# Attention into a three-way-max FFN on one core: weight conversion in three steps, and what the ledger books

## The chip, the cores and the metric

The kernel runs on one core of a Trainium2 chip. Its time is the device time of one execution in microseconds (us), taken from the start of the program to its end. Runs of the same kernel are compared by their median; the trace comes from one execution under the hardware profiler, whose own time stands beside its span below. The core has TensorE (PE in the profile, PEld for its weight loads), VectorE (DVE), ScalarE (ACT), GpSimd (POOL) and SyncE (SP), which here issues all DMA transfers.

## The reference

A local attention with some global tokens, followed by a feed-forward network. There are 8 batches and 8 heads of 512 local and 32 global tokens, of 64 elements each. A local token attends to the 32 global tokens and to the local ones at most 32 places away; a global token attends to all 544.

```python
k_all = concatenate([k_g, k_l], axis=2);  v_all = concatenate([v_g, v_l], axis=2)
out_g = sm(scale * q_g @ k_all.T) @ v_all
s_ll  = where(abs(i - j) <= 32, scale * q_l @ k_l.T, -1e9)
s_lg  = scale * q_l @ k_g.T
out_l = sm(concatenate([s_lg, s_ll], -1)) @ v_all          # sm: softmax
x     = concatenate([out_g, out_l], axis=2)                # to 4608 tokens x 512
h     = maximum(maximum(x @ w1, x @ w2), x @ w3)           # 512 x 768 weights
out   = h @ w_out                                          # 768 x 512
```

All is float32, apart from the four weight arrays, which are float64 in the memory.

## The kernel before

**Precision.** Nearly every product is made of three TensorE products in the fast float32 format (`F32R`): each operand is split into a high part (a cast to `F32R`) and a low part (the operand less the high part), and high x high, high x low and low x high are added in PSUM. A split thus is a cast (`copy`, lines L100 or L102) and a subtraction (`sub`, L94). The first 28 score tiles and 26 probability tiles are instead computed in plain float32 with one product (`NATK`, `NAT`).

**Attention.** A tile `sl` is 128 local queries of a pair `p` of heads; there are 4 tiles a pair (`t`), 16 a batch and 128 in all. For a tile, `scores` makes two score halves on PE (L307 plain, L311 split); a custom DVE operation (L314) adds the mask and takes the maximum `nm`; ACT takes the exponential with its sum (L316); the reciprocal (L318, L319) and a scaling (`times`, L108 DVE, L110 ACT or L112 POOL) give the probabilities `s`, which go through a DMA (L322) to a buffer `early` (tiles up to 15) or `prob`. `trans` transposes them on PE (L334) and splits the result into `pt`; `transg` does so for the global tokens' probabilities (L355); `pv` multiplies by V (L375 plain, L382 split) into `xr`. `glob` and `glob_soft` are scores and softmax of the global queries of the next pair: PE at L265 and L269, DVE's maximum `nmg` at L273. `split_k`, `split_q` and `split_v` make the parts of K, Q and V.

**FFN.** Once the four pairs of a batch are done, `split_x` splits the FFN's input, and `moe_local(b - 1)` is worked off in small portions of matmuls (`fill(4)`, `fill(4)`, `fill(3)`, `fill(7)`) between the steps of the attention tiles of the next batch. For each of 6 column blocks f there are 36 matmuls (L413) with maxima on DVE (L421), then come 4 x 18 matmuls with `w_out` (L432). After the last tile the FFN of the last batch and of the global tokens follows alone.

**Weights.** There are 24 pieces of 128 x 512: 18 of w1, w2, w3 (three for each f) and 6 of `w_out`. A piece is loaded as raw 64-bit words (`wraw`, L162), and `convert` makes a float32 of it by bit operations: ACT's absolute value (L167), then four DVE operations (L168 to L171) into `cut` or, for `w_out`, `wct`; then the high part `wh` or `woh` by `copy` and the low part `wl` or `wol` by `sub`. `convert` is a generator, and `weight_step` moves it on: two steps a piece, and one step carries the second half of one piece and the first of the next. The table `WS` gives the number of steps behind each of tiles 0 to 25.

**What sets the order.** Three things. `copy`, `sub` and `times` choose their engine by a ledger: `load` holds the ns booked for ACT, DVE and POOL, `least` takes the engine with the smallest sum, `spend` books the work that has a fixed engine, and `settle` limits how far an engine can fall behind. Second, each engine works off its own list in order, as the program is written; up to the transpose of tile 16 (`EARLY`) the scheduler of the framework orders the instructions by its own rules. Third, buffers are reused, so a load waits for the last reader of what lay there: `wraw` shares its buffers with the FFN's `h`, `kraw` has one buffer and `kst` two.

Of the kernel before, what the change touches and what calls it, by code (L numbers as in the profile page):

```python
# [10 lines left out]
F32R = mybir.dt.float32r  # L11
# [3 lines left out]
ALU = mybir.AluOpType  # L15
# [4 lines left out]
DM, DF = 512, 768  # L20
# [27 lines left out]
def f32(ap):  # L48
    return ap.bitcast(F32)


def body(ctx, tc, kin, qin, vin, min_, w1, w2, w3, w4, out):
# [23 lines left out]
    def spend(e, ns):  # L76
        load[e] += ns
# [18 lines left out]
    def copy(out, a, psum=False):  # L96
        n = width(out)
        c = {"d": n * (1.04 if psum else 0.52) + (160 if psum else 150), "a": n * 0.833 + (150 if psum else 190)}
        if least(c) == "d":
            dve.tensor_copy(out=out, in_=a)  # L100
        else:
            act.copy(out=out, in_=a)  # L102
# [32 lines left out]
    wo = []  # L135
# [3 lines left out]
    def pieces():  # L139
        n = 0  # L140
        for f in range(12):
            for i in range(3 if f < 6 else 1):
                if f < 6:
                    src = (w1, w2, w3)[i][:, f * 128:(f + 1) * 128].rearrange("(k p) f -> p k f", p=128)
                    yield src, 4, n, wh[f][:, i].rearrange("p k f -> p (k f)"), wl[f][:, i].rearrange("p k f -> p (k f)")
                else:
                    if f == 6:
                        wo.extend(const.tile([128, 6, DM], F32R, name=t, tag=t) for t in ("woh", "wol"))
                    yield w4[(f - 6) * 128:(f - 5) * 128], 1, n, wo[0][:, f - 6], wo[1][:, f - 6]
                n += 1  # L150

    def STAGE(n):
# [5 lines left out]
    def convert(piece):  # L158
        src, k, m, dh, dl = piece
        n, i = 512, STAGE(m)  # L160
        r = moe.tile([128, n], mybir.dt.int64, name="wraw", tag=f"h{i}")
        nc.sync.dma_start(out=r.rearrange("p (k f) -> p k f", k=k) if k > 1 else r, in_=src)  # L162
        hi = r.bitcast(I32).rearrange("p (n t) -> p n t", t=2)[:, :, 1]
        lo = r.bitcast(I32).rearrange("p (n t) -> p n t", t=2)[:, :, 0]
        yield
        c = cut[:, m % 6] if m < 18 else moe.tile([128, n], I32, name="wct", tag="o", bufs=2)
        act.activation(out=f32(c), in_=r.bitcast(F32).rearrange("p (n t) -> p n t", t=2)[:, :, 1], func=AF.Abs)  # L167
        dve.tensor_scalar(out=f32(c), in0=f32(c), scalar1=2.0 ** -15, scalar2=HIMAX, op0=ALU.max, op1=ALU.min)  # L168
        dve.tensor_scalar(out=c, in0=c, scalar1=0x07FFFFFF, scalar2=3, op0=ALU.bitwise_and, op1=ALU.logical_shift_left)
        dve.scalar_tensor_tensor(out=hi, in0=hi, scalar=-0x40000000, in1=c, op0=ALU.bitwise_and, op1=ALU.bitwise_or)  # L170
        dve.scalar_tensor_tensor(out=c, in0=lo, scalar=29, in1=hi, op0=ALU.logical_shift_right, op1=ALU.bitwise_or)  # L171
        spend("a", 520)
        spend("d", 1900)
        yield
        copy(dh, f32(c))
        sub(dl, f32(c), f32(dh))
        yield

    todo = pieces()
    live = []  # L180
# [8 lines left out]


    def weight_step():
        if live:
            next(live.pop())
        if loaded:
            live.append(loaded.pop(0))
            next(live[0])
        weight_load()


# [54 lines left out]
    def glob(p, step):  # L254
        if p >= B * NP:
            return
        if step == 0:
            pg[p] = [att.tile([64, KW], F32, name="sg", bufs=1)[:, 0:NG], small.tile([64, 2], F32, name="nmg"), small.tile([64, 2], F32, name="zg")]
        s, nm, z = pg[p]
        c0, n = SEG[step]  # L260
        s0 = 384 * step
        ps = psS.tile([128, 512], F32, name="S")
        if 4 * p in NATK:

            pe.matmul(ps[0:64, 0:n], lhsT=kraw[p][:, KW:KW + 2 * SG], rhs=kraw[p][:, c0:c0 + n], start=True, stop=True)  # L265
            in1 = zero[0:64].to_broadcast([64, n])
        else:
            for j in range(2):
                pe.matmul(ps[:, 0:n], lhsT=qgz.rearrange("p j x -> p (j x)")[:, 128 * j:128 * j + 128],  # L269
                          rhs=kst[p][:, j, c0:c0 + n], start=(j == 0), stop=(j == 1))  # L270
            in1 = s[:, s0:s0 + n]
            copy(in1, ps[64:128, 0:n], True)
        dve.tensor_tensor_reduce(out=s[:, s0:s0 + n], in0=ps[0:64, 0:n], in1=in1, scale=-0.125, scalar=3.0e38,  # L273
                                 op0=ALU.add, op1=ALU.min, accum_out=nm[:, step:step + 1])
        spend("d", n * 1.04 + 75)

    def glob_soft(p):
        if p >= B * NP:
# [13 lines left out]
    def scores(sl):  # L292
        if sl >= NS:
            return
        p, t = divmod(sl, 4)
        c0, n = WIN[t]

        ps = pm.tile([128, 512], F32, name="pm") if sl < 12 else psS.tile([128, 512], F32, name="S")
        s = att.tile([128, 2, 224], F32, name="s", bufs=4)
        sc[sl] = early[:, sl % 6] if sl < EARLY else prob[sl % 2]  # L300
        nm = small.tile([128, 2], F32, name="nm")
        z = small.tile([128, 2], F32, name="z")
        ph = [ps[:, 0:224], ps[:, 224:448]]
        for j in range(2):
            if sl in NATK:

                pe.matmul(ph[j][:, 0:n], lhsT=qraw[sl][:, 128 * j:128 * j + 128], rhs=kraw[p][:, c0:c0 + n],  # L307
                          start=True, stop=True)
                continue
            for a in range(2):  # L310
                pe.matmul(ph[j][:, 0:n], lhsT=qs[sl][:, a, 128 * j:128 * j + 128],  # L311
                          rhs=kst[p][:, j, c0:c0 + n], start=(a == 0), stop=(a == 1))
        for j in range(2):
            dve.tensor_tensor_reduce(out=s[:, j, 0:n], in0=ph[j][:, 0:n], in1=mask[:, (1, 0, 1, 0)[t], 32 * (t == 0):32 * (t == 0) + n],  # L314
                                     scale=-0.125, scalar=3.0e38, op0=ALU.add, op1=ALU.min, accum_out=nm[:, j:j + 1])
            act.activation(out=s[:, j, 0:n], in_=s[:, j, 0:n], func=AF.Exp, bias=nm[:, j:j + 1], scale=-1.0,  # L316
                           accum_out=z[:, j:j + 1])
        dve.tensor_scalar(out=z, in0=z, scalar1=1e-9, scalar2=None, op0=ALU.add)  # L318
        dve.reciprocal(out=z, in_=z)  # L319
        for j in range(2):  # L320
            times(s[:, j, 0:n], s[:, j, 0:n], z[:, j:j + 1])
        nc.sync.dma_start(out=f32(sc[sl])[:, :, 0:n], in_=s[:, :, 0:n])  # L322
        spend("d", 2 * (n * 1.04 + 75) + 150)
        spend("a", 2 * (n * 0.833 + 278))

    def trans(sl):
# [171 lines left out]
    for sl in range(NS):  # L498
        p, t = divmod(sl, 4)
# [5 lines left out]
        trans(sl + 1)  # L505
        fill(4)
        next_scores(max(min(sl + 5, EARLY - 1), sl + 3))
        if t == 3:
            split_k(p + 2)
            load_k(p + 3)  # L510
        fill(4)
# [72 lines left out]
```

## Time and profile before

| | |
|---|---|
| median of 3 runs | 871.46 us (870.19 to 872.28) |
| the profiled execution's own time | 868.76 us |
| its span | 867.0 us |
| mean granted TensorE clock | 0.968 of full speed |
| busy: PE | 817.3 us, 94% |
| busy: DVE | 617.3 us, 71% |
| busy: ACT | 492.0 us, 57% |
| busy: POOL | 502.9 us, 58% |
| chain that ended last | PE 77%, DVE 10%, DMA 6% |

The busy times are shares of the whole span. The span has three parts: up to about 85 us there is attention alone and weights are converted; up to about 757 us attention tiles and FFN matmuls alternate; the last 110 us are FFN alone. In rows of the timeline the start in us comes first, then the duration, the engine, the line and the operation, and in brackets the idle time of the engine before it and what ended that. In rows of groups the busy time in us and the mean duration in ns stand behind the count.

### The profile page before, as it was taken

To read this page: it belongs to the slowest core of one execution; us is meant where nothing else is said; L and a number is where in the kernel's file an instruction comes from. 1 tells how busy PE (TensorE), PEld (TensorE's weight loads), DVE (VectorE), ACT (ScalarE), POOL (GpSimd) and SP (SyncE) were. 2 spreads that over 40 slices of the span, in tenths; PEclk is the share of its full clock that TensorE was granted. 3 is DMA by queue.
4 is the path that set the end of the run, shared out by engine and by line. 5 is a ranking of instruction groups with operands and counts; after the bars stand their busy time and mean duration, and the time that the engine had idled before them with its cause. 6 is when DMAs were issued, how large, how long until landed. Compare 5 with 4: busy or idle time off the path is not lost.

```text
span 867.0 us, 15698 instructions
## 1 busy us (share of the span) xinstructions
PE 817.3 (94%) x4452; PEld 677.3 (78%) x4452; DVE 617.3 (71%) x1885; ACT 492.0 (57%) x1392; POOL 502.9 (58%) x669
## 2 busy tenths in 40 slices
PE   5865988799999999999999999999999999999997
PEld 3643766588888788888887888888888888888897
DVE  4678897887788787887788887877877877521111
ACT  3654655566666566766666666666666666411111
POOL 4544657576667666776767666756677665411211
PEclk8876889899999999999999999999999999999999
DMA  6676755334333533343333433353333422100000
GB/s 202 192 222 197 212 182 158 117 93 144 99 101 104 160 110 105 99 133 114 103 107 104 142 102 98 101 161 104 111 110 122 122 78 74 62 24 1 25 25 25
DMA packets 107238, 98.53 MB, mean 114 GB/s; under 512 B 21008, under 2 KB 97936, under 8 KB 107152
## 3 DMA queue, kind: packets, MB, share of 16 engines
q1 hardware_dynamic: 107152, 97.53, 37.0%
q8 instruction: 36, 0.59, 0.3%
q14 instruction: 50, 0.41, 0.2%
HBM read 56.85 MB, written 8.91 MB: 76 GB/s over the span
## 4 chain that ended last, share of the span: by engine, by line
PE 77%; DVE 10%; DMA 6%; issue 2%; POOL 2%; ACT 1%; SPq 1%; DVEq 0%; POOLq 0%; ACTq 0%
PE pm L413 45%; PE pm L432 13%; PE O L382 6%; PE S L311 5%; PE T L334 3%; DMA wraw<-w_in 1%; DMA wraw<-wo_in 1%; PE S L269 1%; DVE wraw L170 1%; DVE xs L100 1%; PE S L265 1%; PE S L355 1%; PE O L375 1%; DVE s L314 1%; DVE kst L94 1%
## 5 line engine op out<-in xcount | busy, mean ns | idle before, releaser
L413 PE MATMUL pm<-xs,wh 128*128 128x512 f32 (+1 forms) x1296 | 411.2, 390 | 0.0
L413 PEld LDWEIGHTS pm<-xs,wh 128*128 128x128 f32 x1296 | 235.3, 191 | 31.6
L413 PE MATMUL pm<-xs,wl 128*128 128x512 f32 (+1 forms) x648 | 254.9, 393 | 0.0
L112 POOL TENSOR_SCALAR s<-s,z 128x224 f32<-128x224 f32 (+1 forms) x243 | 111.6, 472 | 87.7 <-ACT lox L102 46.7
L316 ACT ACTIVATE s<-s,nm 128x192 f32<-128x192 f32 (+1 forms) x256 | 118.0, 462 | 48.6 <-DVE nm L314 44.0
L413 PEld LDWEIGHTS pm<-xs,wl 128*128 128x128 f32 x648 | 123.6, 191 | 23.5 <-issue 2.4
L432 PE MATMUL pm<-woh,h 128*128 128x512 f32 x408 | 135.2, 400 | 1.3 <-POOL h L94 1.1
L94 POOL TENSOR_TENSOR h<-m,h 128x512 fp32r<-128x512 f32 (+1 forms) x54 | 69.3, 1284 | 99.2 <-ACT h L102 99.2
L94 POOL TENSOR_TENSOR qs<-qraw,qs 128x256 fp32r<-128x256 f32 x100 | 79.5, 795 | 68.6 <-ACT qs L102 42.0
L421 DVE TENSOR_TENSOR m<-pm,m 128x512 f32<-128x512 f32 (+1 forms) x108 | 71.0, 657 | 63.0 <-PE pm L413 62.7
L94 DVE TENSOR_TENSOR pt<-T,pt 128x512 fp32r<-128x512 f32 x102 | 70.4, 691 | 36.2 <-ACT pt L102 33.8
L432 PEld LDWEIGHTS pm<-woh,h 128*128 128x128 f32 x408 | 74.6, 188 | 15.4 <-POOL h L94 4.3
L314 DVE CUSTOM_DVE_ANT_0 s<-S,mask 128x192 f32<-128x192 f32 (+1 forms) x232 | 77.5, 370 | 9.9 <-PE S L307 5.2
L432 PE MATMUL pm<-wol,h 128*128 128x512 f32 x204 | 81.7, 401 | 0.0
L94 POOL TENSOR_TENSOR vs<-vraw,vs 128x256 fp32r<-128x256 f32 x102 | 75.7, 743 | 9.0 <-ACT vs L102 4.2
L102 ACT CAST pt<-T 128x512 fp32r<-128x512 f32 x83 | 48.4, 583 | 47.6 <-PE T L334 47.6
L382 PEld LDWEIGHTS O<-pt,vs 128*128 128x128 f32 x408 | 66.4, 188 | 9.2
L382 PE MATMUL O<-pt,vs 128*128 128x320 f32 (+1 forms) x408 | 72.8, 299 | 0.0
L102 ACT CAST qs<-qraw 128x256 fp32r<-128x256 f32 x85 | 34.6, 407 | 64.3 <-PE S L311 64.0
L334 PEld LDWEIGHTS T<-identr,prob 128*128 128x128 f32 x448 | 51.3, 143 | 24.9 <-issue 5.0
L311 PEld LDWEIGHTS S<-kst,qs 128*128 128x128 f32 x400 | 59.5, 190 | 11.2 <-DVE nmg L273 2.8
L102 ACT CAST h<-m 128x512 fp32r<-128x512 f32 (+1 forms) x54 | 32.3, 597 | 60.5 <-DVE m L421 60.4
(99 smaller groups left out, 1340.5 us busy)
## 6 DMA issues: line engine op xcount, KB each, us to landing
vraw<-v_in SPq DMA_DIRECT2D x128, 128.0 KB, 2.6
qraw<-q_in SPq DMA_DIRECT2D x100, 128.0 KB, 2.2
prob<-s SPq DMA_DIRECT2D x56, 224.0 KB, 2.4
prob<-s SPq DMA_DIRECT2D x56, 192.0 KB, 2.3
wraw<-w_in SPq DMA_DIRECT2D x18, 512.0 KB, 4.5
out_dram<-o SPq DMA_DIRECT2D x32, 256.0 KB, 2.6
kraw<-k_in SPq DMA_DIRECT2D x25, 320.0 KB, 3.1
qn<-q_in SPq DMA_DIRECT2D x28, 128.0 KB, 3.5
```

The source lines that it names most:

```text
L94: (dve if least(c) == "d" else pool).tensor_tensor(out=out, in0=a, in1=b, op=ALU.subtract)
L100: dve.tensor_copy(out=out, in_=a)
L102: act.copy(out=out, in_=a)
L112: pool.tensor_scalar(out=out, in0=a, scalar1=col, scalar2=1.0, op0=ALU.mult, op1=ALU.mult)
L311: pe.matmul(ph[j][:, 0:n], lhsT=qs[sl][:, a, 128 * j:128 * j + 128], rhs=kst[p][:, j, c0:c0 + n], start=(a == 0), stop=(a == 1))
L314: dve.tensor_tensor_reduce(out=s[:, j, 0:n], in0=ph[j][:, 0:n], in1=mask[:, (1, 0, 1, 0)[t], 32 * (t == 0):32 * (t == 0) + n], scale=-0.12 ...
L316: act.activation(out=s[:, j, 0:n], in_=s[:, j, 0:n], func=AF.Exp, bias=nm[:, j:j + 1], scale=-1.0, accum_out=z[:, j:j + 1])
L334: i = pe.transpose(pr[:, 256 * j + 128 * c:256 * j + 128 * c + 128], s[:, j, 128 * c:128 * c + 128], identr)
L382: pe.matmul(o[:, j, 0:320].rearrange("p (a q) -> p a q", a=2)[:, :, 0:n], lhsT=vs[sl][:, 2 * j + c].rearrange("p a d -> p (a d)"), rhs=pt[ ...
L413: pe.matmul(ps[:, 0:n], lhsT=w[f][:, i, k], rhs=xs[k][:, a, 0:n], start=(q == 0), stop=(q == 11))
L421: dve.tensor_tensor(out=m[:, 0:n], in0=ps[:, 0:n], in1=m[:, 0:n], op=ALU.max)
L432: pe.matmul(ps, lhsT=hh[f][:, a, 128 * t:128 * t + 128], rhs=w[:, f], start=(q == 0), stop=(q == 17))
```

## The change

Three things are changed.

`convert` now has three steps behind the load: ACT's absolute value; the four DVE operations and the high part, which is always a DVE cast; the low part, which is always a POOL subtraction. `weight_step` moves on every piece that is under way by one step. The pair of tiles for `w_out` is made at the first DVE step that needs it.

The ledger books more for DVE in `scores` (for a tile of width n, 2 x (1.04 n + 220) + 440 instead of 2 x (1.04 n + 75) + 150, which is 580 ns more) and in `glob` (145 ns more); for a piece it books 650 ns on ACT, 2800 on DVE and 1350 on POOL as the steps come.

`split_k(p + 2)` and `load_k(p + 3)` stand at the third tile of a pair instead of the fourth.

```diff
@@ convert
         yield
         c = cut[:, m % 6] if m < 18 else moe.tile([128, n], I32, name="wct", tag="o", bufs=2)
         act.activation(out=f32(c), in_=r.bitcast(F32)..., func=AF.Abs)
+        spend("a", 650)
+        yield
         dve.tensor_scalar(out=f32(c), in0=f32(c), scalar1=2.0 ** -15, scalar2=HIMAX, op0=ALU.max, op1=ALU.min)
         dve.tensor_scalar(out=c, in0=c, scalar1=0x07FFFFFF, scalar2=3, ...)
         dve.scalar_tensor_tensor(out=hi, in0=hi, scalar=-0x40000000, in1=c, ...)
         dve.scalar_tensor_tensor(out=c, in0=lo, scalar=29, in1=hi, ...)
-        spend("a", 520)
-        spend("d", 1900)
+        if m >= 18:
+            if not wo:
+                wo.extend(const.tile([128, 6, DM], F32R, name=t, tag=t) for t in ("woh", "wol"))
+            dh, dl = [w[:, dh] for w in wo]
+        dve.tensor_copy(out=dh, in_=f32(c))
+        spend("d", 2800)
         yield
-        copy(dh, f32(c))
-        sub(dl, f32(c), f32(dh))
-        yield
+        pool.tensor_tensor(out=dl, in0=f32(c), in1=f32(dh), op=ALU.subtract)
+        spend("p", 1350)
+        yield True
@@ weight_step
-        if live:
-            next(live.pop())
+        for c in live[:]:
+            if next(c, True):
+                live.remove(c)
         if loaded:
             live.append(loaded.pop(0))
-            next(live[0])
+            next(live[-1])
         weight_load()
@@ glob
-        spend("d", n * 1.04 + 75)
+        spend("d", n * 1.04 + 220)
@@ scores
-        spend("d", 2 * (n * 1.04 + 75) + 150)
+        spend("d", 2 * (n * 1.04 + 220) + 440)
@@ the loop over tiles
-        if t == 3:
+        if t == 2:
             split_k(p + 2)
             load_k(p + 3)
```

In the changed kernel the conversion stands at L165 (absolute value), L168 to L171, L176 (high part) and L180 (low part), and lines from `scores` on have numbers higher by 6.

By count over the whole program DVE has fewer instructions (1808 instead of 1887), ACT more (1171 instead of 1106) and POOL more (688 instead of 674); PE and SP have as many as before. On DVE there are 24 high parts of weights instead of 6; in return K's casts go from 24 to 4, K's subtractions from 7 to 0, Q's casts from 15 to 0 and V's from 17 to 7.

Three places show how rows move. First DVE around the scores of tile 16 (the two halves of width 192). Before, from the second half on:

```order
L314 ISA s,nm<-S,mask 128x192
L314 ISA nm 128x1
L273 ISA sg,nmg<-S,zero 64x160
L273 ISA nmg 64x1
L281 TENSOR_TENSOR nmg<-nmg 64x1
L168 TENSOR_SCALAR cut<-cut 128x512
L169 TENSOR_SCALAR cut<-cut 128x512
L318 TENSOR_SCALAR z<-z 128x2
L314 ISA s,nm<-S,mask 128x224
L314 ISA nm 128x1
L170 SCALAR_TENSOR_TENSOR wraw<-wraw,cut 128x512
L319 RECIPROCAL z<-z 128x2
```

and now:

```order
L320 ISA s,nm<-S,mask 128x192
L320 ISA nm 128x1
L279 ISA sg,nmg<-S,zero 64x160
L279 ISA nmg 64x1
L287 TENSOR_TENSOR nmg<-nmg 64x1
L324 TENSOR_SCALAR z<-z 128x2
L325 RECIPROCAL z<-z 128x2
L320 ISA s,nm<-S,mask 128x224
L320 ISA nm 128x1
L168 TENSOR_SCALAR cut<-cut 128x512
```

The sum and the reciprocal `z` of tile 16 now follow each other directly; three conversion operations and a half of the next tile that stood between or ahead of them come later.

The second place is PE where the FFN starts, from the P·V of tile 16 on. Before:

```order
L375 MATMUL O<-pt,vraw 64x160 x4
L334 MATMUL T<-identr,prob_93 128x128 x4
L413 MATMUL pm<-xs,wh_102 128x512 x2
L413 MATMUL pm<-xs,wl_108 128x512
L413 MATMUL pm<-xs,wh_102 128x512 x2
L355 MATMUL S<-identr,probg_94 128x128
```

and now:

```order
L381 MATMUL O<-pt,vraw 64x160 x4
L419 MATMUL pm<-xs,wh_102 128x512 x2
L419 MATMUL pm<-xs,wl_108 128x512
L419 MATMUL pm<-xs,wh_102 128x512 x2
L419 MATMUL pm<-xs,wl_108 128x512
L419 MATMUL pm<-xs,wh_102 128x512 x2
L419 MATMUL pm<-xs,wl_108 128x512
L419 MATMUL pm<-xs,wh_102 128x512 x2
L419 MATMUL pm<-xs,wl_108 128x512
L419 MATMUL pm<-xs,wh_102 128x512 x2
L340 MATMUL T<-identr,prob_93 128x128 x4
```

Fourteen FFN matmuls have moved ahead of the transpose of tile 17 (`prob_93`).

The third place is DVE at the first split tiles, 155 to 163 us in the trace. Before:

```order
L314 ISA nm 128x1
L100 CAST qs<-qraw 128x256
L100 CAST kst<-kraw 64x576
L94 TENSOR_TENSOR kst<-kraw,kst 64x576
L318 TENSOR_SCALAR z<-z 128x2
L100 COPY sg<-S 64x384
L319 RECIPROCAL z<-z 128x2
L100 CAST vs<-vraw 128x4x64
L108 TENSOR_SCALAR s<-s,z 128x192 x2
L273 ISA sg,nmg<-S,sg 64x384
```

and now:

```order
L320 ISA nm 128x1
L169 TENSOR_SCALAR wct<-wct 128x512
L170 SCALAR_TENSOR_TENSOR wraw<-wraw,wct 128x512
L171 SCALAR_TENSOR_TENSOR wct<-wraw 128x512
L324 TENSOR_SCALAR z<-z 128x2
L279 ISA sg,nmg<-S,sg 64x384
L279 ISA nmg 64x1
L176 CAST woh<-wct 128x512
```

The casts of Q, K and V, K's subtraction, the copy of the global scores and the scaling have left DVE here; three conversion operations of a `w_out` piece stand in their place.

More of the change, by code (lines that the diff above doesn't have):

```diff
@@ L146, in pieces @@
                 else:
-                    if f == 6:
-                        wo.extend(const.tile([128, 6, DM], F32R, name=t, tag=t) for t in ("woh", "wol"))
-                    yield w4[(f - 6) * 128:(f - 5) * 128], 1, n, wo[0][:, f - 6], wo[1][:, f - 6]
+                    yield w4[(f - 6) * 128:(f - 5) * 128], 1, n, f - 6, None
                 n += 1
```

## The prediction

> **What bounds the kernel now.** I read three views. First the busy tenths of the page, 40 slices of 21.7 us:
>
> ```profile
> PE   5865988799999999999999999999999999999997
> DVE  4678897887788787887788887877877877521111
> PEclk8876889899999999999999999999999999999999
> ```
>
> From the ninth slice on TensorE is at nine tenths in every slice but the last, at full clock. Before it PE is at five to eight tenths and its clock dips three times. So the question is what the first 180 us do, and whether the rest keeps its cover. The second view is a table of stretches (window, length, busy us of PE, PEld, DVE, ACT, POOL with their instruction counts, granted clock, DMA share, GB/s):
>
> ```profile
> 70.00:90.00 20.00, 12.61 (x67) 9.43 (x65) 17.81 (x44) 12.10 (x34) 9.47 (x9) 0.67 0.62 194
> 90.00:115.00 25.00, 23.77 (x128) 17.81 (x127) 22.31 (x53) 14.43 (x37) 16.14 (x17) 0.96 0.75 230
> 135.00:155.00 20.00, 17.82 (x99) 13.27 (x98) 13.44 (x38) 10.75 (x28) 13.30 (x15) 1.00 0.48 148
> 155.00:163.70 8.70, 6.08 (x36) 4.76 (x37) 8.54 (x18) 3.84 (x12) 7.55 (x7) 1.00 0.39 119
> 163.70:170.50 6.80, 4.69 (x15) 3.22 (x14) 5.67 (x18) 3.28 (x11) 2.56 (x5) 0.50 0.24 72
> 600.00:700.00 100.00, 99.70 (x551) 83.95 (x550) 81.55 (x256) 66.05 (x190) 68.11 (x93) 1.00 0.37 112
> ```
>
> In the last row PE idles 0.3 of 100 us: work moved from DVE to ACT or POOL is worth nothing there, whatever its size. In 70 to 90 PE idles 7.39 of 20 us at clock 0.67 while DVE is 89% busy; in 155 to 163.7 PE idles 2.62 us while DVE is 98% busy; behind that come 6.8 us at half clock. The third view, PE's waits in 70 to 200 us (total, times, longest), says what ends them, and the timeline where:
>
> ```profile
> PE T L334 <- DMA prob<-s: 8.0, 3, 4.5
> PE S L355 <- DVE nm L314: 3.0, 2, 2.1
> PE S L269 <- DVE nmg L273: 1.9, 1, 1.9
> ...
> 79.94 0.72 PE L334 MATMUL T<-identr,prob 128*128 128x128 f32 x4 [4.50 <-DMA prob<-s]
> 86.43 0.72 PE L334 MATMUL T<-identr,prob 128*128 128x128 f32 x4 [2.89 <-DMA prob<-s]
> 86.95 1.18 PE L413 MATMUL pm<-xs,wh 128*128 128x512 f32 x2
> 148.20 0.26 PE L355 MATMUL S<-identr,probg 128*128 128x128 f32 x1 [2.06 <-issue]
> 155.73 0.28 PE L355 MATMUL S<-identr,probg 128*128 128x128 f32 x1 [0.85 <-DVE nm L314]
> 162.94 0.46 PE L269 MATMUL S<-kst,qgz 128*128 128x160 f32 x2 [1.89 <-DVE nmg L273]
> 166.50 0.37 PE L355 MATMUL S<-identr,probg 128*128 128x128 f32 x1 [2.11 <-DVE nm L314]
> ```
>
> Two places carry the prediction: the two transposes at 79.94 and 86.43, which wait for a probability tile to come back through DMA before the FFN's first matmul at 86.95, and the three waits on DVE at 155.73, 162.94 and 166.50, together 4.85 us. PE waits there for maxima that DVE reaches late, because conversions and splits lie before them in its queue.
>
> **The change, part by part.** The sum is made against the profiled execution's own 868.76 us; the median of the runs, 871.46, lies 2.70 above it, and I add that at the end.
>
> *Tile 16's probabilities (the 4.50 us wait).* Its scale factor is made here:
>
> ```profile
> 73.76 0.43 DVE L168 TENSOR_SCALAR cut<-cut 128x512 f32<-128x512 f32 x1
> 73.98 0.19 ACT L316 ACTIVATION_READ_ACCUMULATOR s<-s,nm 128x1 f32 x1
> 75.55 0.16 DVE L319 RECIPROCAL z<-z 128x2 f32<-128x2 f32 x1
> 75.87 1.54 POOL L112 TENSOR_SCALAR s<-s,z 128x192 f32<-128x192 f32 x2 [5.95 <-ACT cut L167]
> ```
>
> ACT's sum is there at 74.17, yet the reciprocal starts at 75.55, behind two conversion operations, another tile's score half and a third conversion operation. In the new order sum and reciprocal follow each other at once: 74.17 plus an addition, which I take as long as the reciprocal's 0.16, is 74.3, so 1.2 us earlier. POOL had been idle 5.95 us and starts at once. Two casts more ahead of tile 16's scores, by the counts of the two orders, cost 0.3 net. I take -0.9; ends -1.8 (from 73.76) and 0.
>
> *The FFN ahead of tile 17's transpose (the 2.89 us wait).* Fourteen FFN matmuls now stand ahead of that transpose. At the 0.59 us of the row at 86.95 they last 8.3 us, which covers 2.89 wholly. What is late next: tile 17's transpose, by up to 8.3 - 2.89 = 5.4 us, and with it its P·V and what DVE copies from it. DVE is 89% busy in the stretch behind (22.31 of 25), so not all of it stays. I take -2.0; ends -2.9 and 0.
>
> *DVE at 155 to 163 us.* What stands between the tile's last maximum and the global one:
>
> ```profile
> 155.59 0.82 DVE L100 CAST qs<-qraw 128x256 fp32r<-128x256 f32 x1
> 156.33 0.99 DVE L100 CAST kst<-kraw 64x576 fp32r<-64x576 f32 x1
> 157.35 1.74 DVE L94 TENSOR_TENSOR kst<-kraw,kst 64x576 fp32r<-64x576 f32 x1
> 159.74 0.56 DVE L100 COPY sg<-S 64x384 f32<-64x384 f32 x1
> 160.29 1.03 DVE L100 CAST vs<-vraw 128x256 fp32r<-128x256 f32 x1
> 161.25 1.05 DVE L108 TENSOR_SCALAR s<-s,z 128x192 f32<-128x192 f32 x2
> ...
> 159.76 1.41 POOL L94 TENSOR_TENSOR kst<-kraw,kst 64x576 fp32r<-64x576 f32 x1
> ...
> L169 DVE TENSOR_SCALAR wct<-wct 128x512 int32<-128x512 int32 x6 | 2.7, 444 | 0.1
> L170 DVE SCALAR_TENSOR_TENSOR wraw<-wraw,wct 128x512 int32<-128x512 int32 x6 | 4.1, 682 | 0.0
> L171 DVE SCALAR_TENSOR_TENSOR wct<-wraw 128x512 int32<-128x512 int32 x6 | 5.5, 914 | 0.0
> ```
>
> All six leave DVE at this place: 0.82 + 0.99 + 1.74 + 0.56 + 1.03 + 1.05 = 6.19. Three steps of a weight piece come in: 0.44 + 0.68 + 0.91 = 2.04. DVE is 4.15 us earlier at the global maximum, which covers 0.85 + 1.89 and 1.4 of the 2.11 behind them. What is late next is POOL: it is busy 7.55 of 8.70, and one K subtraction more, 1.41 by its own row, is 0.26 more than its room of 1.15. ACT has room (3.84 of 8.70) for the casts. Splitting K one tile sooner gives POOL a tile more time for it; the order leaves the K loads and the last three weight loads at their places among SP's transfers, so that by itself I price at nothing. If that cover is gone, one subtraction of 1.41 stands in front of the scores. I take -4.15 + 0.26 = -3.9; ends -4.85 and 0.
>
> *The half clock behind it.* In 163.7 to 170.5 PE's 4.69 busy us ran at 0.50; at full clock they are 2.35. The dip follows the waits of 1.89 and 2.11; but the 2.06 at 148.20 was followed by none (1.00 in 135 to 155), so shorter waits don't decide it alone. I take half, -1.2; ends -2.35 and 0.
>
> [...]
>
> *Batch boundaries.* There, in 200 to 760 us, PE waits on the subtraction of h and on a global maximum:
>
> ```profile
> PE pm L432 <- POOL h L94: 1.1, 2, 0.9
> PE S L311 <- DVE nmg L273: 0.8, 3, 0.3
> ```
>
> K's cast and subtraction leave DVE in front of these, but the subtraction goes to POOL, in front of h. Ends -1.9 (both waits gone) and +1.4 (one subtraction ahead of one h). I take -1.0, since POOL is a third free in the steady rows (68.11 of 100).
>
> *More casts on DVE.* Eighteen pieces' high parts leave ACT for DVE; some twelve of them fall in 73 to 135 us, where DVE has least room:
>
> ```profile
> L168 DVE TENSOR_SCALAR cut<-cut 128x512 f32<-128x512 f32 x18 | 12.9, 718 | 3.5 <-ACT cut L167 3.4
> L100 DVE CAST wh<-cut 128x512 fp32r<-128x512 f32 x6 | 2.5, 420 | 0.1
> L100 DVE COPY xr<-O 128x160 f32<-128x160 f32 x5 | 1.6, 321 | 1.1 <-PE O L375 1.0
> 111.01 3.00 DVE L168 TENSOR_SCALAR cut<-cut 128x512 f32<-128x512 f32 x1
> ...
> 112.44 1.28 POOL L94 TENSOR_TENSOR wl<-cut,wh 128x512 fp32r<-128x512 f32 x1
> ```
>
> 12 x 0.42 = 5.04, less four xr copies of 0.32 that leave it, is 3.7 us more. DVE's idle time in the first two stretches is 2.19 + 2.69 = 4.9, part of it waiting for scores that come sooner now, so a third is absorbed and I take +2.5. The lower end is 0 (all absorbed). For the upper end: the L168 step takes 0.43 alone and 0.718 on average, so each cast may be stretched by the same 0.29 beside a running POOL; 12 x (0.42 + 0.29) - 1.3 = +7.2, nothing absorbed.
>
> *Free edits.* That ACT no longer stands still for a cut, and that a piece takes a step more, cost and gain nothing: by the table of steps, pieces finish at least a tile before the FFN asks for their column block, and no FFN matmul waits for a weight in the list of PE's waits.
>
> Sum: -0.9 - 2.0 - 3.9 - 1.2 - 1.0 + 2.5 = -6.5, so 862.3 for a profiled execution and **865.0** as the median.
>
> **The rivals.** *A, the waits change hands.* PE gets to the FFN earlier, but the scores come no sooner since DVE sets them (89% in 70 to 115), and what PE saves at 86 and 162 it waits for later. Then tile 16, tile 17, the DVE place and the clock give 0, the casts fall into PE's waits, the boundaries -1.0: 870.5, no change. For it: DVE's share. Against it: at 155 to 163 work really leaves DVE.
>
> *B, DVE's queue from 73 to 135 us becomes the bound: slower.* Place: the score maxima between the conversions. Price: +7.2, as above; PE then waits for probabilities and both early gains are gone; -3.9 and -1.0 stay: +2.3, or **873.8**. It decides from the point where DVE is more than 3.9 + 1.0 = 4.9 us late at 135. For it: the 3.00 us of one L168 while POOL was at work; against it: the order puts the score halves of tiles 17 and 18 nearer together, with fewer conversion steps between.
>
> [...]
>
> *C, everything at its end.* The clock stays up, both early waits and all boundary waits go, the casts are absorbed: -1.8 - 2.9 - 4.85 - 2.35 - 1.9 = -13.8, or **857.7**. For it: 7.39 us of idle PE at 0.67 in one stretch. Against it: six things at once.
>
> **How the numbers follow.** Chances: the forecast 0.55, A 0.17, B 0.16, C 0.12. The forecast's own range is 860 to 869 (the DVE place and the casts half of their way to their ends). The range of 857 to 875 takes in C and B up to 1 us past its price; outside it remain the tails of both. What can be told from no change is 0.2%, 1.7 us: the forecast, C and a small part of A (0.01) are faster, 0.68; the rest of A is the same, 0.16; B is slower, 0.16.
>
> **What would show it.** In the changed profile: FFN matmuls ahead of tile 17's transpose, no wait of 2.9 us there, and the first wait below 4.50 by about 0.9. Between 150 and 170 us no wait of PE on a maximum above 1 us, DVE below 90%, and the clock at 1.00 instead of 0.50. DVE from 70 to 115 at most 3 us busier. From 600 to 700 us the same 99.7 busy us of PE. It would be wrong if PE's waits in 90 to 135 us exceeded 5 us, if K's subtraction on POOL released a score matmul, or if one of the new casts took over 1 us on average.

## The result and the profile after

The changed kernel takes 862.30 us (median; 861.51 to 863.21), the kernel before 870.83 in the same comparison: a ratio of 0.9902, with a 95% interval of 0.9881 to 0.9923. That is 8.5 us faster. The forecast was 865.0 with a range of 857 to 875, so sign and size came out. The way there did not, as the profile after shows. Its profiled execution took 862.75 us, 6.0 less than the one before; the two spans, on which the stretches below are measured, are 867.0 and 860.8 us. First the busy tenths:

```profile
PE   5857888899999999999999999999999999999997
DVE  5567999677777677776777777867787776511111
PEclk8886999999999999999999999999999999999999
```

The clock of the fifth, sixth and eighth slice is now at nine tenths. DVE is fuller than before in the fifth and seventh slice, and mostly emptier from the eighth on. The same stretches as in the prediction, one more (115 to 135), and the last two rows, which are the clock's dips behind 92 us:

```profile
70.00:90.00 20.00, 15.38 (x81) 10.95 (x82) 13.83 (x40) 10.79 (x32) 10.58 (x11) 0.81 0.59 174
90.00:115.00 25.00, 22.31 (x125) 16.21 (x123) 23.26 (x58) 12.37 (x34) 15.41 (x16) 1.00 0.68 208
115.00:135.00 20.00, 15.20 (x73) 10.46 (x73) 19.76 (x41) 9.41 (x26) 13.10 (x13) 0.91 0.68 202
155.00:163.70 8.70, 8.70 (x52) 6.81 (x50) 6.96 (x14) 5.38 (x15) 5.70 (x6) 0.93 0.26 81
163.70:170.50 6.80, 4.58 (x27) 3.43 (x24) 5.03 (x16) 2.88 (x10) 4.28 (x7) 1.00 0.50 150
600.00:700.00 100.00, 100.00 (x556) 84.82 (x556) 74.91 (x242) 73.12 (x209) 70.81 (x98) 1.00 0.36 111
118.60:122.00 3.40, 3.40 (x10) 2.25 (x8) 3.33 (x7) 1.87 (x5) 3.03 (x5) 0.50 0.33 78
152.70:156.10 3.40, 3.40 (x11) 2.93 (x11) 0.75 (x2) 2.01 (x4) 1.27 (x1) 0.51 0.81 265
```

PE gained in 70 to 90 (15.38 busy instead of 12.61) and in 155 to 163.7 (8.70 of 8.70 instead of 6.08). It lost between them: from 115 to 135 DVE is busy 19.76 of 20 us and PE idles 4.8. And from 600 to 700 PE has no idle time at all. The dips are not gone: where the kernel before has two of 6.8 us behind 92 us, this one has two of 3.4. One of the two before is the stretch 163.7 to 170.5 of the prediction; the other is

```profile
115.90:122.70 6.80, 6.18 (x19) 5.23 (x20) 5.79 (x12) 3.99 (x11) 3.69 (x5) 0.50 0.48 165
```

To say how much each stretch gave, one needs the same point of the program in both traces. In the first 205 us I take PE's transposes of tiles 20, 24 and 33, called A, B and C: ahead of each, PE has carried out the same number of instructions in every run (418, 562 and 861). In the kernel before and in the changed one:

```profile
108.58 0.46 PE L334 MATMUL T<-identr,prob 128*128 128x128 f32 x4
141.30 0.51 PE L334 MATMUL T<-identr,prob 128*128 128x128 f32 x4
205.25 0.46 PE L334 MATMUL T<-identr,prob 128*128 128x128 f32 x4
...
108.75 0.46 PE L340 MATMUL T<-identr,prob 128*128 128x128 f32 x4
142.07 0.45 PE L340 MATMUL T<-identr,prob 128*128 128x128 f32 x4
204.08 0.46 PE L340 MATMUL T<-identr,prob 128*128 128x128 f32 x4
```

Behind that, DVE's sum of a pair's global rows (`xg`) serves, which comes once a pair, at its end. There are 32; the eighth, 27th, 28th and 31st of the kernel before, and the eighth and 31st of the changed one:

```profile
204.91 0.40 DVE L392 TENSOR_REDUCE xg<-xr 128x32 f32<-128x128 f32 x1
648.06 0.39 DVE L392 TENSOR_REDUCE xg<-xr 128x32 f32<-128x128 f32 x1
672.04 0.39 DVE L392 TENSOR_REDUCE xg<-xr 128x32 f32<-128x128 f32 x1
741.37 0.40 DVE L392 TENSOR_REDUCE xg<-xr 128x32 f32<-128x128 f32 x1
...
203.72 0.39 DVE L398 TENSOR_REDUCE xg<-xr 128x32 f32<-128x128 f32 x1
735.48 0.39 DVE L398 TENSOR_REDUCE xg<-xr 128x32 f32<-128x128 f32 x1
```

In the first 200 us these sums are no measure of PE: before, the fourth starts at 89.73, though PE's last product for it was done by 83.54; in the changed kernel it starts at 86.64, behind a product done by 83.82. The 3.1 us between them are the order of DVE's queue. The second execution in the table is a later trace of the changed kernel (e5 below).

| stretch | before | changed | difference | second execution | its difference | forecast for it |
|---|---|---|---|---|---|---|
| start to A | 108.58 | 108.75 | +0.2 | 106.48 | -2.1 | -0.4 up to B (tile 16, FFN ahead of tile 17, casts) |
| A to B | 32.72 | 33.32 | +0.6 | 32.98 | +0.3 | in the line above |
| B to C | 63.95 | 62.01 | -1.9 | 62.26 | -1.7 | -5.1 (DVE place, clock) |
| C to the end | 661.7 | 656.7 | -5.0 | 656.8 | -5.0 | -1.0 (batch boundaries) |

From the eighth to the 31st pair's end alone it is 536.46 before and 531.76 now, 4.7 us less. Four fifths of the gain of the first trace, and more than half of that of the second, thus lie behind C, where the prediction saw 1 us. The single pairs show what went there. Before, most of these 23 pairs take 23.0 to 23.2 us, but the 12th, 13th, 16th, 19th, 24th and 28th take 23.6 to 24.05, and the 20th 23.4; they lie at the ends of the batches of four pairs or next to them. Now every one takes 23.05 to 23.22.

PE's waits from 80 to 175 us in the changed kernel, from the timeline (the longer ones):

```profile
81.79 0.51 PE L340 MATMUL T<-identr,prob 128*128 128x128 f32 x4 [2.00 <-DMA prob<-s]
86.64 0.50 PE L419 MATMUL pm<-xs,wh 128*128 128x512 f32 x1 [0.56 <-ACT xs L102]
88.00 0.51 PE L419 MATMUL pm<-xs,wh 128*128 128x512 f32 x1 [0.85 <-POOL xs L94]
95.29 0.28 PE L361 MATMUL S<-identr,probg 128*128 128x128 f32 x1 [1.62 <-DVE nm L320]
...
117.24 0.51 PE L340 MATMUL T<-identr,prob 128*128 128x128 f32 x4 [2.17 <-DMA prob<-s]
...
134.01 0.28 PE L361 MATMUL S<-identr,probg 128*128 128x128 f32 x1 [1.74 <-DVE nm L320]
...
151.93 0.25 PE L361 MATMUL S<-identr,probg 128*128 128x128 f32 x1 [3.77 <-DMA probg<-sg]
167.26 0.28 PE L361 MATMUL S<-identr,probg 128*128 128x128 f32 x1 [2.23 <-DVE nm L320]
```

Where waits of 4.50 and 2.89 stood before the FFN, there are now 2.00 and two of 0.56 and 0.85 on the FFN's own input. New waits stand at 95, 117 and 134, and the one at 166 is still there, at 167.26. Ahead of this stretch, too, there is a longer one than before: 3.52 us up to 71.20, where it was 2.72 up to 68.12.

### The profile page after: what moved, and what is told of

It reads as the page before. It is cut to its first block, busy times and chain, and to the rows that moved or that the text cites. A ratio compares the mean times of both kernels' runs of the same rounds, so it can differ in the third digit from the quotient of the medians.

```text
span 860.8 us, 15729 instructions
## 1 busy us (share of the span) xinstructions
PE 809.9 (94%) x4452; PEld 673.8 (78%) x4452; DVE 577.0 (67%) x1806; ACT 517.2 (60%) x1457; POOL 509.9 (59%) x683
## 4 chain that ended last, share of the span: by engine, by line
PE 83%; DVE 7%; DMA 5%; SPq 2%; issue 2%; ACT 1%; POOL 1%; DVEq 0%; ACTq 0%; POOLq 0%
PE pm L419 46%; PE pm L438 17%; PE O L388 7%; PE S L317 5%; PE T L340 4%; DVE wraw L170 2%; PE S L275 1%; DMA wraw<-w_in 1%; DMA probg<-sg 1%; DMA prob<-s 1%; DVE cut L171 1%; PE S L361 1%; PE pm L313 1%; SPq L296 1%; DMA early<-s 1%
## 5 line engine op out<-in xcount | busy, mean ns | idle before, releaser
L419 PEld LDWEIGHTS pm<-xs,wh 128*128 128x128 f32 x1296 | 234.1, 190 | 34.3 <-POOL xs L94 1.2
L112 POOL TENSOR_SCALAR s<-s,z 128x192 f32<-128x192 f32 (+1 forms) x249 | 113.4, 468 | 86.4 <-ACT lox L102 36.8
L94 POOL TENSOR_TENSOR h<-m,h 128x512 fp32r<-128x512 f32 (+1 forms) x54 | 67.5, 1250 | 96.2 <-ACT h L102 96.1
L94 POOL TENSOR_TENSOR qs<-qraw,qs 128x256 fp32r<-128x256 f32 x100 | 73.9, 749 | 54.9 <-ACT qs L102 41.2
L324 DVE TENSOR_SCALAR z<-z 128x2 f32<-128x2 f32 x128 | 55.0, 430 | 50.9 <-ACT s L322 50.2
L94 POOL TENSOR_TENSOR kst<-kraw,kst 64x576 fp32r<-64x576 f32 x50 | 71.9, 1439 | 11.8 <-issue 8.3
L102 ACT CAST pt<-T 128x512 fp32r<-128x512 f32 x91 | 53.2, 585 | 40.2 <-PE T L340 39.9
L102 ACT CAST qs<-qraw 128x256 fp32r<-128x256 f32 x100 | 40.7, 407 | 49.8 <-PE S L317 48.1
```

Source lines behind the costliest of these rows:

```text
L94: (dve if least(c) == "d" else pool).tensor_tensor(out=out, in0=a, in1=b, op=ALU.subtract)
L112: pool.tensor_scalar(out=out, in0=a, scalar1=col, scalar2=1.0, op0=ALU.mult, op1=ALU.mult)
L419: pe.matmul(ps[:, 0:n], lhsT=w[f][:, i, k], rhs=xs[k][:, a, 0:n], start=(q == 0), stop=(q == 11))
```

## The experiments

The questions were: which part of the change gives the gain behind 205 us, which gives or takes in the first 200, and what the weight steps cost there. Times are medians in us; runs with the same letter were compared with the same runs of the kernel before.

| run | what it is | us | before | ratio (95%) |
|---|---|---|---|---|
| e1 | bookings alone | 865.81 | 869.96 (a) | 0.9946 (0.9924 to 0.9967) |
| e2 | earlier K split alone | 876.84 | (a) | 1.0081 (1.0058 to 1.0104) |
| e3 | three steps alone | 868.65 | (a) | 0.9986 (0.9975 to 0.9998) |
| e4 | bookings and K split | 860.22 | (a) | 0.9881 (0.9860 to 0.9901) |
| e5 | the changed kernel again | 861.61 | 869.34 (b) | 0.9911 (0.9896 to 0.9926) |
| e6 | e4 again | 859.73 | (b) | 0.9888 (0.9875 to 0.9902) |
| e7 | changed, high part on ACT | 859.20 | (b) | 0.9885 (0.9869 to 0.9901) |
| e8 | K always off DVE, K split earlier | 862.74 | (b) | 0.9920 (0.9905 to 0.9935) |
| e9 | changed, late weight loads | 860.53 | 870.38 (c) | 0.9879 (0.9861 to 0.9896) |
| e10 | e4 with high parts on DVE | 862.73 | (c) | 0.9913 (0.9896 to 0.9930) |
| e11 | e2 with Q's casts on ACT | 868.58 | (c) | 0.9981 (0.9971 to 0.9992) |
| e12 | e7, first FFN input's low parts on DVE | 854.76 | (c) | 0.9821 (0.9804 to 0.9839) |

From their profiled executions, the same stretches by PE's transposes, and the 8th to the 31st pair (us):

| run | to A | A to B | B to C | 8th to 31st pair |
|---|---|---|---|---|
| before | 108.6 | 32.7 | 64.0 | 536.5 |
| changed / e5 | 108.8 / 106.5 | 33.3 / 33.0 | 62.0 / 62.3 | 531.8 / 531.8 |
| e1 | 110.8 | 33.5 | 60.9 | 534.9 |
| e2 | 107.0 | 32.8 | 63.9 | 549.9 |
| e3 | 106.1 | 35.1 | 64.7 | 536.0 |
| e4 / e6 | 105.3 / 106.1 | 32.1 / 32.1 | 61.2 / 62.9 | 532.2 / 531.7 |
| e7 | 109.0 | 30.5 | 60.6 | 531.7 |
| e8 | 107.8 | 32.8 | 62.9 | 533.9 |
| e9 | 107.8 | 34.6 | 59.2 | 531.9 |
| e10 | 105.4 | 34.1 | 64.0 | 531.7 |
| e11 | 106.4 | 34.3 | 63.5 | 538.1 |
| e12 | 105.1 | 30.1 | 61.1 | 531.6 |

Two executions of one kernel agree within 0.5 us in the last column and within 0.4 from A to B, but differ by up to 2.3 up to A and by up to 1.7 from B to C; the kernel before was traced once. What is said below of the first 205 us therefore goes by the medians, and by stretches only where several runs agree.

### The parts alone (e1 to e4)

e1, the bookings alone:

```diff
-        spend("d", n * 1.04 + 75)
+        spend("d", n * 1.04 + 220)
-        spend("d", 2 * (n * 1.04 + 75) + 150)
+        spend("d", 2 * (n * 1.04 + 220) + 440)
```

> The kernel before with the two bookings alone (580 ns more a score tile, 145 ns more a global part). Theory L: the bookings alone keep PE full from 200 to 757 us, since they send K's casts and subtractions, the FFN input's and Q's casts from DVE to ACT and POOL at each batch's last pair; that stretch gets 4.9 us shorter as in the changed kernel, the first 200 us move by less than 2 us: 866 us. Rival S (the earlier split of K does it): within 1.5 us of before, 870 us. Rival W (the weight steps do it): also 870 us.

e2, the split alone:

```diff
-        if t == 3:
+        if t == 2:
             split_k(p + 2)
             load_k(p + 3)
```

> The kernel before with K split and loaded one tile sooner, nothing else. Theory L: DVE still gets its K splits, PE still idles about 2.5 us between 200 and 757 us, so 870 us, within 1.5 us. Rival S: the split no longer meets the last pair's work of a batch, the 4.9 us between 200 and 757 us are gained here: 866 us.

e3 is the change without these two edits, e4 the change without the three steps (`convert` and `weight_step` as before).

> The changed kernel with the old bookings in scores and the global part and the K split at its old place: only the three weight steps are left. The prediction's early terms (tile 16, the FFN ahead of tile 17, the casts) belong to the steps: -0.9 - 2.0 + 2.5, so 870 us within 2 us, with the wait for tile 17's probabilities gone. Theory L: 200 to 757 us unchanged. Rival W: 866 us or less.

> The changed kernel with the old two weight steps: new bookings and earlier K split alone. If the parts add up this is the bookings' gain plus that of the split: theory L 865 to 867 us, with the waits of 2.9 us at tile 17 and 4.5 us at tile 16 still there. If the three steps bring nothing, 862 us as the changed kernel; if they cost time beside the others, below 862 us.

The bookings give half of the gain, 4.1 us. The split alone costs 6.9. The steps alone give 1.3. But bookings and split together give 9.7, more than the whole change. So the parts don't add up: the split is worth -5.6 with the new bookings and +6.9 with the old ones. The last column says the same in one stretch: the bookings alone shorten it by 1.6, not by the 4.9 that theory L expected, the split alone lengthens it by 13.4, and both together shorten it by 4.3 to 4.8. Theory L had the median of e1 right, but not the stretch; the traced execution of e1 is 1.1 us above its median, so where the rest of the 4.1 lies isn't seen. For e2 both theories were wrong, L with no change and S with 866 us; its traced execution is the longest of its six, 3.3 above the median. e3 came out as expected, within 2 us of 870 and with tile 17's wait gone. In e4 the waits of 4.5 and 2.9 us that were expected to stay at tiles 16 and 17 are down to 1.64 and 0.61, though it lacks the three steps, and at 860.22 it is below 862: the steps cost time beside the other two parts.

The groups of K, Q and the FFN input on DVE between 205 and 757 us show how. Before:

```profile
L100 DVE CAST kst<-kraw 64x576 fp32r<-64x576 f32 x22 | 18.6, 846 | 0.2
L100 DVE CAST xs<-xr 128x512 fp32r<-128x512 f32 x12 | 10.3, 877 | 0.1
L100 DVE CAST qs<-qraw 128x256 fp32r<-128x256 f32 x12 | 8.8, 735 | 0.0
L94 DVE TENSOR_TENSOR kst<-kraw,kst 64x576 fp32r<-64x576 f32 x5 | 8.7, 1737 | 0.2
```

With the whole change:

```profile
L100 DVE CAST kst<-kraw 64x576 fp32r<-64x576 f32 x4 | 5.0, 1248 | 0.1
L100 DVE CAST xs<-xr 128x512 fp32r<-128x512 f32 x4 | 3.9, 981 | 0.0
```

With the split alone, and then PE's waits there:

```profile
L100 DVE CAST qs<-qraw 128x256 fp32r<-128x256 f32 x25 | 30.9, 1235 | 0.4
L100 DVE CAST kst<-kraw 64x576 fp32r<-64x576 f32 x22 | 18.3, 831 | 0.5
L94 DVE TENSOR_TENSOR kst<-kraw,kst 64x576 fp32r<-64x576 f32 x5 | 9.5, 1895 | 0.2
...
PE S L311 <- DVE nmg L273: 10.7, 5, 2.3
```

With the old bookings the split moved K's parts on DVE to another tile, where the ledger then gave DVE 13 more casts of Q, each longer (1235 ns instead of 735), and PE waited 10.7 us for global maxima behind them. In three places the clock went to 0.50 behind such a wait, for 3.4 to 6.8 us (its mean from 205 to 757 us is 0.99, before 1.00), so the stretch lost more than the 10.7. With new bookings and split DVE has no cast of Q left there and four of K's. In e1, with the bookings alone, PE waits 1.5 us in 4 for probabilities instead, and its trace shows on what:

```profile
372.57 0.17 DVE L319 RECIPROCAL z<-z 128x2 f32<-128x2 f32 x1
373.28 2.94 POOL L94 TENSOR_TENSOR kst<-kraw,kst 64x576 fp32r<-64x576 f32 x2
376.31 0.83 POOL L112 TENSOR_SCALAR s<-s,z 128x192 f32<-128x192 f32 x2
379.61 0.51 PE L334 MATMUL T<-identr,prob 128*128 128x128 f32 x4 [0.44 <-DMA prob<-s]
```

The scale factor `z` is there at 372.74, but POOL first works off K's two subtractions and scales at 376.31. The prediction had put +1.4 on one such subtraction in POOL's queue, ahead of h; here two hold up the probabilities. With the split one tile sooner as well, PE has no wait left in this stretch.

### Is it K or Q? (e8 and e11)

e8 forces K off DVE with the split one tile sooner; all else is as before, the old bookings too:

```diff
-        copy(t[0:64, 0], r[0:64, 0:KW])
-        copy(t[64:128, 1], r[64:128, 0:KW])
-        sub(t[64:128, 0], r[0:64, 0:KW], f32(t)[0:64, 0])
-        sub(t[0:64, 1], r[64:128, 0:KW], f32(t)[64:128, 1])
+        for o, i in (...):          # (...): left out here; the two high parts
+            spend("a", 670)
+            act.copy(out=o, in_=i)
+        for o, i, h in (...):       # the two low parts
+            spend("p", 1470)
+            pool.tensor_tensor(out=o, in0=i, in1=h, op=ALU.subtract)
```

> The kernel before with K's casts always on ACT, K's subtractions always on POOL, and the K split one tile sooner; bookings of scores and weight steps as before. Theory K (of the bookings' effect it is K's split that counts): PE full from 200 to 757 us, that stretch 4 to 5 us shorter, so 865 us. Rival Q (Q's, V's and the FFN input's casts on DVE matter too): the DVE room that K leaves is filled by those casts, which the ledger then gives to DVE; PE still waits for maxima, 868 us or more.

e11 is e2 with `copy(t[:, 0], r)` of `split_q` replaced by `spend("a", 405)` and `act.copy`.

> The kernel before with the K split one tile sooner, and Q's casts always on ACT. The split alone cost 6.9 us, and in its profile 25 casts of Q on DVE of 1.2 us each stand ahead of the global maxima for which PE waits 10.7 us between 200 and 757 us. Theory Q: those casts are the cost; without them no more than 870 us, and PE's waits on the global maximum below 3 us. Rival K: it is K's casts and subtractions at their new place (22 and 5 on DVE, as before); then 874 us or more.

K off DVE gives 6.6 us without any change of the bookings, 2.6 of it behind 205 us: of the bookings' and the split's joint 4.7 there, K is a little over half. Theory K had named 865 us and 4 to 5 for that stretch, rival Q a median of 868 or more; neither is wholly right. e11 is 8.3 us faster than the split alone (868.58 against 876.84), more than the split had cost, so Q's casts were that cost. But PE's waits on the global maximum are still there, 4.9 us in 5, above the 3 us expected, and the last column stays 1.7 above the kernel before. In e8 DVE still makes 23 casts of Q in that stretch, and its list of PE's waits has none on the global maximum; with K on DVE and Q off it, in e11, there is one. So with the early split K's parts are what stands ahead of the global maximum. That Q's must leave as well for the whole 4.7 is not shown: no run takes both off DVE by hand.

### What the three steps cost (e5 to e7, e9, e10)

> The changed kernel once more, beside the next one. Theory P (the three steps cost time next to the other two parts, through DVE's casts and longer conversions in 85 to 150 us): 862 us, 2 us above the kernel without the steps, and between the end of the first batch's attention (some 87 us) and 150 us it loses 4 to 5 us against the kernel before, as in the first profile. Rival N (the two are equal; the difference lay in the chip or in one execution): within 0.7 us of the next one.

> Bookings and earlier K split without the three steps, once more. Theory P: 860 us, 2 us below the changed kernel, and ahead of the kernel before by 6 us at 205 us. Rival N: within 0.7 us of the changed kernel, and ahead by less than 3 us at 205 us.

e7 gives the high part back to ACT, in the third step, with its booking:

```diff
-        dve.tensor_copy(out=dh, in_=f32(c))
-        spend("d", 2800)
+        spend("d", 2380)
         yield
+        act.copy(out=dh, in_=f32(c))
+        spend("a", 620)
```

> The changed kernel with one thing undone: the high part of every piece is an ACT cast in the third step, ahead of POOL's subtraction. Theory P, if it is DVE's twenty-four casts that cost: 12 x 0.42 to 0.59 us less DVE work in 73 to 165 us, some 6 us, of which PE gets 2 to 4 back: 859 to 860 us. Rival O (it is the order of the three steps, with low parts later on POOL and a weight load ahead of a probability transfer on SP): 862 us, unchanged.

e10 does the opposite in the kernel without the steps: `copy(dh, f32(c))` becomes `spend("d", 420)` and `dve.tensor_copy`.

> Bookings and earlier K split with the old two steps, but every high part on DVE. Theory P: the casts cost here as they do in three steps, 861.5 to 862 us, 2 us above the same kernel with high parts chosen by the ledger (859.7), with DVE busier in 85 to 150 us by 4 to 9 us. Rival O (order of three steps): 859.7 us, no change.

The changed kernel is 1.9 us behind the one without the steps when both run side by side. Taking the high parts off DVE wins 2.4 back (0.9911 to 0.9885), and putting them on DVE in the old two steps loses as much (0.9888 to 0.9913, 2.2 us). The intervals of each two overlap somewhat (e10 and e6 also come from different comparisons), but all three (e5 with e6, e5 with e7, e10 with e6) point the same way by about the same amount. The stretch from A to B says it too, like against like: 33.0 us in e5 and 30.5 in e7, 32.1 in e6 and 34.1 in e10. Two things came out otherwise than expected. e6 was to be ahead of the kernel before by 6 us at 205 us and is 4.2 ahead at C (e4 6.7). And the 4 to 5 us that e5 was to lose from some 87 to 150 us stand between DVE's sums alone (64.7 us from the fourth to the sixth, 59.5 before); by PE's transposes there is +0.3 from A to B.

DVE's share between 85 and 150 us, changed kernel, e10, e7 and e6 in that order:

```profile
85.00:150.00 65.00, 54.26 (x283) 39.10 (x281) 62.49 (x143) 33.65 (x92) 43.40 (x43) 0.97 0.59 179
...
85.00:150.00 65.00, 52.65 (x276) 39.56 (x277) 60.12 (x136) 32.20 (x89) 42.94 (x41) 0.93 0.57 178
...
85.00:150.00 65.00, 52.98 (x281) 38.37 (x281) 53.37 (x125) 38.93 (x101) 40.78 (x41) 0.97 0.58 180
...
85.00:150.00 65.00, 56.93 (x300) 41.87 (x300) 51.60 (x130) 39.16 (x103) 42.05 (x43) 0.95 0.59 183
```

With the casts DVE is busy 60 to 62 of 65 us, without them 52 to 53. ACT, which did them before, is at 33 and 39 of 65. The casts themselves take, in the changed kernel between 85 and 150 us:

```profile
L176 DVE CAST wh<-cut 128x512 fp32r<-128x512 f32 x10 | 6.1, 607 | 0.0
L176 DVE CAST woh<-wct 128x512 fp32r<-128x512 f32 x4 | 2.4, 608 | 0.0
```

Fourteen casts are 8.5 us, and 9.1 is what lies between DVE's busy time here and in e7: the casts account for nearly all of it.

e9 leaves the casts and lets the loads from the twenty-first weight piece on come one step later (one empty `weight_load`). Its reason is SP's queue in the changed kernel:

```profile
127.82 1.02 POOL L112 TENSOR_SCALAR s<-s,z 128x192 f32<-128x192 f32 x2 [0.39 <-ACT wct L165]
...
130.13 0.33 SPq L160 DMA_DIRECT2D wraw<-wo_in  x1
130.56 0.64 SPq L328 DMA_DIRECT2D prob<-s  x1
```

> The changed kernel with the loads from the twenty-first weight piece on issued one weight step later; DVE's casts stay. In the changed kernel SP stands at that load until DVE is done with the piece whose buffer it takes (issued at 130.13 us), and the transfer of a probability tile that POOL had ready at 128.8 is issued behind it at 130.56. Theory P (DVE's casts cost the 2 us): 861.6 us as the changed kernel, within 0.7 us, since PE waits for DVE's maxima there anyway. Rival SP (the queue costs it): 860 us or less.

In e9 POOL scales from 126.59 to 127.61, and the transfer is issued at 127.64. The median is 1.1 us lower than that of e5, the ratio 0.9879 against 0.9911, which is 2.8 us, with intervals that just touch at 0.9896. That is more than theory P's 0.7 and in the sense of rival SP, whose 860 us it misses by 0.5. But the profiled execution of e9 is no further at C (201.58 us) than that of e5 (201.72), and PE still waits 1.84 us on DVE's maximum, at 132.78. Whether the queue costs 1 us, or 3, or nothing beside DVE, stays open; in e7 the transfer isn't held up either, so a part of e7's 2.4 us may be this.

### A version that beats both (e12)

In e7 PE waited for the FFN's first input, with POOL's row behind it:

```profile
91.74 0.50 PE L420 MATMUL pm<-xs,wh 128*128 128x512 f32 x1 [3.64 <-POOL xs L94]
...
88.11 1.92 POOL L112 TENSOR_SCALAR s<-s,z 128x224 f32<-128x224 f32 x2 [2.22 <-DVE z L326]
90.00 1.69 POOL L94 TENSOR_TENSOR xs<-xr,xs 128x512 fp32r<-128x512 f32 x1
```

e12 gives the low parts of the first batch's input to DVE:

```diff
-        sub(d[1], src, f32(d[0]))
+        if 0 in xs:
+            spend("d", 690)
+            dve.tensor_tensor(out=d[1], in0=src, in1=f32(d[0]), op=ALU.subtract)
+        else:
+            sub(d[1], src, f32(d[0]))
```

> The kernel with three steps and high parts on ACT, and the low parts of the first FFN input on DVE instead of POOL. In its profile PE waited 3.64 us at 91.74 for the last of these low parts, which lay in POOL's queue behind two low parts of weights and a scaling. If that wait sets what follows: 857 us, 2 us below. If DVE, which is full from 90 to 150 us, only hands it on: 859 us, no change.

It takes 854.76 us, 0.9821 (0.9804 to 0.9839) of the kernel before: 15.6 us faster than it, and some 7 faster than the changed kernel. Against e7 it is 4.4 us by the medians and 5.6 by the ratios, more than the 2 that the better of its two expectations named. In its profile PE has no wait between 79 and 92 us. At A it is 3.9 us ahead of e7, at C 3.8 (196.32 against 200.10): what is gained before the FFN starts is kept, although DVE got work for it.

## Why the prediction came out, and where it was wrong

**What bounds the kernel.** From the row 600 to 700 us, where PE idles 0.3 of 100, the prediction read that work moved off DVE is worth nothing there, and it took the idle time in PE's waits, 1.9 us, for the most that the batch boundaries can give. This is the step that failed. The whole stretch of the kernel before:

```profile
205.00:757.00 552.00, 549.49 (x3027) 463.09 (x3026) 442.17 (x1389) 361.50 (x1032) 367.08 (x503) 1.00 0.36 110
```

PE idles 2.5 of 552 us, yet the kernel before was 4.7 us slower there, nearly twice its idle time. In the very row 600 to 700 lies the 28th pair, 23.98 us long before (the two `xg` rows above) and 23.22 now: 0.8 us behind an idle time of 0.3. The rest lies in rows that count as busy. In this stretch a matmul starts 0.23 us after the one before, while its row lasts 0.39 (two in one row last 0.62); a wait therefore costs 0.16 more than the idle time listed, and a start that comes up to 0.16 late leaves no idle time at all. Added up over the starts of PE's matmuls from the eighth to the 31st pair, whatever came over 0.03 us later than is usual for the same two operations is 4.5 us more in the kernel before than in the changed one. That is the 4.7.

**Batch boundaries, -1.0: measured -4.7 from the eighth to the 31st pair.** The mechanism was the one named (K's parts leave DVE in front of the global maximum and h), with Q's casts beside it; the size was off, and its lower end of -1.9, taken from the list of waits, was no bound. The price on the other side, a subtraction on POOL ahead of h (+1.4), did not come. e1 and e2 add that neither the bookings nor the split would do it alone (-1.6 and +13.4).

**Tile 16, -0.9, and the FFN ahead of tile 17, -2.0.** The first is not there. POOL starts tile 16's scaling at 78.46 us, and at 76.08 in the second trace, not earlier than the 75.87 before, and PE's transpose of it starts at 81.79 and 79.42 against 79.94. The wait in front of it went from 4.50 to 2.00 since PE came to it later; a shorter wait alone is no gain. The second is there: the FFN starts at 83.75 us (82.07 in the second trace) instead of 86.95. But it is not the steps' alone. Ten to seventeen FFN matmuls stand ahead of tile 17's transpose in every other kernel here, with the split alone (e2) as with the steps alone (e3); only the bookings alone (e1) leave the order as it was. What is left of both terms at A, casts included, is +0.2 in one trace and -2.1 in the other, on both sides of the forecast's -0.4 up to B, so these traces can't tell how large they are. The next thing late, the FFN's own input (1.41 us), the prediction had not named; e12 shows that it was worth following up.

**Casts on DVE, +2.5: measured 2.2 to 2.4 by e7 and e10.** The price was right and so was the place, rival B's. A cast took 0.61 us on average between 85 and 150 us, between the 0.42 of the forecast and the 0.42 + 0.29 of its upper end: ten of the fourteen took 0.41 or 0.42, one 0.59 and three 1.19 to 1.36. By PE's transposes the cost lies between A and B, where e7 is 2.5 us shorter than e5 and e10 2.0 longer than e6.

**DVE at 155 to 163 us, -3.9, and the clock, -1.2: measured -1.9 and -1.7 together, from B to C.** DVE fell from 98% to 80% busy from 155 to 163.7 us, and of PE's three waits of 4.85 those of 0.85 and 1.89 went. The third, of 2.11, is still there with 2.23. Part was given back at 151.93, where PE waits 3.77 for the global probabilities, against 2.06 at the same operation before. The clock in 163.7 to 170.5 is 1.00 instead of 0.50, but there is a dip of 3.4 us behind the wait of 3.77, and one of 6.8 us (from 148.8 on) in the second trace. So the clock's term is not borne out: the dip moved, and in one of the two traces it is as long as before. The reading behind that term was wrong, too. The wait of 2.11 ended at 166.50 and began at 164.39, inside the dip, which began at 163.7. Nor does PE's work in the stretch ahead tell a dip. In the 3.40 us before one PE was busy for 1.27 us (112.50 to 115.90) and 1.51 (160.30 to 163.70) in the kernel before, and for 1.36 (115.20 to 118.60) and 0.77 (149.30 to 152.70) in the changed one; but it was busy for only 1.34 from 144.80 to 148.20 in the kernel before, with the wait of 2.06 in it, and the clock stayed at 1.00 up to 163.7. What sets off a dip is not shown here.

**The rivals.** In the first 205 us it was a mixture of the forecast and of rivals A and B: the FFN starts 3.2 us sooner, at A nothing of it is left in the first trace, with DVE at 96% from 85 to 150 us, and 1.9 us are gained from B to C. One of the conditions under which the prediction would be wrong was met: PE's waits in 90 to 135 us, 7.5 us in the timeline, exceed 5; and PE's wait of 2.23 on a maximum at 167.26 is above the 1 us that was to be the most there. That the total fits is luck: the DVE place and the clock gave some 3.3 us less than forecast, while what lies behind C gave 4.0 more. By the medians, the first estimate of -6.5 was 2 us short.

## What to carry to other kernels

Measure a saturated stretch by its repeating unit, not by the idle time of its bound engine: here some pairs that were 0.5 to 0.9 us longer than their neighbours held twice what the list of waits showed. Choose the marks on the engine that sets the time: DVE's sums, read as marks in the first 200 us, would have shown a gain of 3 us that PE didn't have. A wait that gets shorter is a gain only if what follows it starts earlier. A helper that chooses engines by a ledger makes edits depend on each other: the same move of a split cost 6.9 us with one booking and gave 5.6 with another, so parts of such a change have to be timed together as well as alone. When a wait goes, look at what the same engine needs next: the FFN's own input, the next thing late, was worth another 4 to 6 us beside e7.

## What was not expected of the hardware

Executions of one kernel spread in the first 110 us: the changed kernel came to A at 108.75 and at 106.48 us, while from the eighth to the thirty-first pair it took 531.76 and 531.79. A difference below some 2 us in such a start can't be read from one trace. And the clock's dips did not go by the length of one wait: one of 2.06 us, up to 148.20, was followed by none (clock 1.00 from 135 to 155 us), one of 1.89, up to 162.94, by 6.8 us at 0.50 from 163.7 on. PE's busy time in the 3.40 us ahead did not tell them apart either: 1.34 us without a dip, 1.51 with one.
